# Batch 0's attention scores and exponentials kept in their PSUM bank up to the division, in a mixture-of-experts kernel

## Chip, cores, metric

One core of one Trainium2 chip runs the kernel. The metric is the device time of one execution in microseconds (us). The kernel before has a median of 1451.16 us over 3 runs (1449.22 to 1452.23).

## What is computed

Three stages follow one another: banded attention with 8 heads over 2 batches of 768 rows, a mixture of 8 experts whose weights come from a Sinkhorn iteration, and a gated feed-forward layer. Everything is fp32. The change touches the attention alone:

```python
scores = scale * np.matmul(q, k.transpose(0, 1, 3, 2))
...
scores = scores + bias[None, :, :, :]
scores = np.where(keep, scores, -1000000000.0)
scores = scores - np.max(scores, axis=-1, keepdims=True)
a = np.exp(scores)
a = a / (np.sum(a, axis=-1, keepdims=True) + 1e-09)
return np.matmul(a, v).astype(np.float32)
```

A row attends to its 96 nearest predecessors and to 8 global keys, so a tile of 128 queries needs two blocks of keys and 32 columns for the global keys.

## The kernel before

**Tiles.** The attention is cut into 2 batches x 4 pairs of heads x 6 tiles of 128 queries, 48 tiles in all. Tile 0 of a pair has 128 columns of scores for each head, tile 1 has 256, tiles 2 to 5 have 288 (`W`). `attention_banded` (L1084) makes one turn of its loop for each tile, and the letters of `ORDER` (L28) say in which order the steps of a turn are written into the engines' queues. Nothing reorders them afterwards. There are two ways of working: `self.phase` is 1 while attention runs alone (24 tiles of batch 0 and the first two of batch 1, turns 0 to 25), and 2 once the first expert layer's matmuls are interleaved with what is left of the attention.

**A turn of phase 1** has the order `tsvrn`. For turn n:

- `t`, `turn` (L1030), for the tile of turn n-3: PE transposes the weights `a` into the bank `pt` (L1039) and the 32 global columns into `pg` (L1047); ACT copies them to `ah` (L1042) and `ag` (L1051).
- `s`, `scores` (L978), for the tile of turn n, once for each of the pair's two heads j: three matmuls into a bank `s` (L1002); DVE adds the bias, scales and keeps the row's minimum in one pass, `tensor_tensor_reduce` (L1015; the trace calls it CUSTOM_DVE); ACT takes the exponential and sums the row into `rs` (L1018, followed by a read of its accumulator).
- `v`, `values` (L1066), for turn n-4: PE multiplies by the values (L1080), and after every second tile ACT copies the result out (L852).
- `r`: DVE subtracts to get the low part `al` (L1060) of turn n-3's transposed weights.
- `n`, `norm` (L1022), for turn n-1: DVE adds 1e-9 to the two row sums (L1025, called the epsilon step below), takes the reciprocal (L1026) and multiplies each head's weights by it (L1028, the two divisions).

After tiles 1 and 4 of each pair, `prep_qk` (L928) transposes the next half of the keys and queries: PE into `pk`, `pq`, ACT to `kh`, `qh` (L939, L949), DVE to `kl`, `ql` (L940, L950).

**PSUM.** There are eight banks: two for `s`, two for `t`, one for `v`, three for `m`. In phase 1 `psum` (L639) sends the scores to the three `m` banks, which nothing else uses then. A score bank of the kernel before comes free when DVE's pass L1015 has read it, since that pass writes to the SBUF tile `a`.

**POOL** splits the values and, in phase 1, the first expert weights and the first half of the layer's inputs (`split`, L207; `sum_weights`, L193), in one queue that runs beside the turns.

Of the kernel before, what the change touches and what calls it, by code (L numbers as in the profile page):

```python
# [12 lines left out]
ALU = mybir.AluOpType  # L13
# [3 lines left out]
P = 128  # L17
GK = 32
SLOT = P + GK
W = 2 * P + GK  # L20
# [28 lines left out]
class Kernel:  # L49
# [928 lines left out]
    def scores(self, b, hp, i):  # L978

        nc = self.nc  # L980
        qh, ql = self.aq[i // 3]

        pairs = lambda x, step: x.rearrange("p (s k) -> p s k", k=step)[:, :2, :P]
        if i == 0:
            keys, bias, wn = lambda x: x[:, :P], self.bias[:, W + P : W + 2 * P], P
        elif i == 1:
            keys, bias, wn = lambda x: pairs(x, SLOT), pairs(self.bias, W), 2 * P
        else:
            keys, bias, wn = lambda x: x[:, (i - 1) * SLOT : (i - 1) * SLOT + W], self.bias[:, P : P + W], W
        a = self.a_a.tile([P, 2, W], F32, tag="a", name=f"a_{b}_{hp}_{i}")  # L990
        rs = self.a_m.tile([P, 2], F32, tag="rs", name=f"rs_{b}_{hp}_{i}")

        rows = [slice(64 * j, 64 * j + 64) for j in range(2)]
        passes = [(ql, self.kh), (qh, self.kl), (qh, self.kh)]
        ps = {}

        def product(j, n):
            if n == 0:
                ps[j] = self.psum("s", [P, W], f"s_{b}_{hp}_{i}_{j}")[:, :wn]
            o = pairs(ps[j], P) if i == 1 else ps[j]  # L1000
            x, y = passes[n]
            nc.tensor.matmul(o, x[rows[j], i % 3, :], keys(y[rows[j]]), start=(n == 0), stop=(n == 2))  # L1002

        if self.phase > 1:
            for n in range(3):
                for j in range(2):
                    product(j, n)
        for j in range(2):
            if self.phase == 1:
                for n in range(3):  # L1010
                    product(j, n)
            s = a[:, j, :wn]
            o, x = (pairs(s, P), pairs(ps[j], P)) if i == 1 else (s, ps[j])
            m = self.a_m.tile([P, 1], F32, tag="m", name=f"m_{b}_{hp}_{i}_{j}")
            nc.vector.tensor_tensor_reduce(  # L1015
                out=o, in0=x, in1=bias, scale=-self.slope(2 * hp + j), scalar=3.0e38, op0=ALU.add, op1=ALU.min, accum_out=m
            )
            nc.scalar.activation(s, s, AF.Exp, bias=m, scale=-1.0, accum_out=rs[:, j : j + 1])  # L1018
            yield
        self.aa[b, hp, i] = a, rs, wn  # L1020

    def norm(self, b, hp, i):  # L1022
        nc = self.nc
        a, rs, wn = self.aa[b, hp, i]
        nc.vector.tensor_scalar(rs, rs, 1e-9, None, op0=ALU.add)  # L1025
        nc.vector.reciprocal(rs, rs)  # L1026
        for j in range(2):
            nc.vector.tensor_scalar(a[:, j, :wn], a[:, j, :wn], rs[:, j : j + 1], None, op0=ALU.mult)  # L1028

    def turn(self, b, hp, i):  # L1030

# [52 lines left out]
    def attention_banded(self):  # L1084

        nc = self.nc
        self.aq, self.av, self.vg = {}, {}, {}
        self.aa, self.at = {}, {}
        pairs = [(b, hp) for b in range(self.B) for hp in range(self.HP)]
        work = [(b, hp, i) for b, hp in pairs for i in range(self.NT)]  # L1090
        tables = self.tables()
        next(tables)
        self.scales()
        self.counts()
        next(tables)
        yield from self.prep_qk(0)
        next(tables)
        for n in range(len(work) + LV):
            b, hp, i = work[n] if n < len(work) else (None, None, None)
            pair = n // self.NT  # L1100
            rest = None
            for o in ORDER[self.phase]:
                if o == "s" and i is not None:
                    yield from self.scores(b, hp, i)
                    if n == 0:
                        self.prep_v(0)
                if o == "t" and LT <= n < len(work) + LT:
                    rest = self.turn(*work[n - LT])
                if o == "n" and 1 <= n <= len(work):
                    self.norm(*work[n - 1])  # L1110
                if o == "r" and rest is not None:
                    rest()
                    yield
                if o == "v" and n >= LV:
                    self.values(*work[n - LV])
                    yield work[n - LV]
            if i == 1:
                yield from self.prep_qk(2 * pair + 1)
            if i == 4 and pair + 1 < len(pairs):
                yield from self.prep_qk(2 * pair + 2)  # L1120
            if i == 2:
                self.prep_v(2 * pair + 1)
            if i == 5 and pair + 1 < len(pairs):
                self.prep_v(2 * pair + 2)
# [246 lines left out]
```

## Time and profile before

| | us |
|---|---|
| median of 3 runs | 1451.16 |
| the profiled execution | 1449.99 |
| its span, first to last instruction | 1448.2 |
| start of turn 0 on DVE | 12.3 |
| start of turn 26, the first of phase 2 | 97.2 |

The profile shows one execution. "Busy" of an engine is the sum of its instructions' times, and "idle before, <- X" is time in which the engine stood before an instruction until X released it. On DVE and ACT an instruction's time overlaps the next one's by about 0.08 us, so what an instruction costs in a queue is read from one start to the next. Starts in the timelines are us from the first instruction of the span.

### The profile page before, as it was taken

To read this page: it belongs to the slowest core of one execution; us is meant where nothing else is said; L and a number is where in the kernel's file an instruction comes from. 1 tells how busy PE (TensorE), PEld (TensorE's weight loads), DVE (VectorE), ACT (ScalarE), POOL (GpSimd) and SP (SyncE) were. 2 spreads that over 40 slices of the span, in tenths; PEclk is the share of its full clock that TensorE was granted. 3 is DMA by queue.
4 is the path that set the end of the run, shared out by engine and by line. 5 is a ranking of instruction groups with operands and counts; after the bars stand their busy time and mean duration, and the time that the engine had idled before them with its cause. 6 is when DMAs were issued, how large, how long until landed. Compare 5 with 4: busy or idle time off the path is not lost.

```text
span 1448.2 us, 20861 instructions
## 1 busy us (share of the span) xinstructions
PE 1403.7 (97%) x7295; PEld 1239.3 (86%) x7295; DVE 1002.1 (69%) x1881; ACT 638.6 (44%) x1528; POOL 851.6 (59%) x998
## 2 busy tenths in 40 slices
PE   7889999899999999999999999999999998999998
PEld 5568888788898998998998998998998977898997
DVE  7987886667767777777677777777655474556655
ACT  5676766343443343333343333343333365444332
POOL 4745555656885656554666554666554566566642
PEclk9999999999999999999999999999999999999999
DMA  6322210111231222221222221222100100010002
GB/s 160 79 50 63 74 48 30 59 59 59 70 113 59 74 80 88 73 74 51 87 75 87 74 71 54 84 77 88 44 30 29 44 16 30 30 44 30 30 1 88
DMA packets 92627, 89.55 MB, mean 62 GB/s; under 512 B 41824, under 2 KB 70496, under 8 KB 92512
## 3 DMA queue, kind: packets, MB, share of 16 engines
q1 hardware_dynamic: 92512, 88.12, 19.1%
q8 instruction: 60, 0.98, 0.3%
q14 instruction: 55, 0.45, 0.1%
HBM read 76.56 MB, written 11.53 MB: 61 GB/s over the span
## 4 chain that ended last, share of the span: by engine, by line
PE 83%; DVE 10%; ACT 4%; issue 2%; POOL 1%; POOLq 0%; DVEq 0%; ACTq 0%
PE pl L559 41%; PE pl1y L504 11%; PE pl1x L504 11%; PE pl1z L504 10%; PE pl1w L504 5%; PE pv L1080 2%; DVE hl L483 1%; PE s L1002 1%; DVE a L1028 1%; DVE u L456 1%; DVE a L1015 1%; DVE al L1060 1%; PE pt L1039 1%; ACT hh L480 1%; PE plg L374 0%
## 5 line engine op out<-in xcount | busy, mean ns | idle before, releaser
L570 DVE SCALAR_TENSOR_TENSOR acc<-pl,pr,acc 128x512 f32<-128x512 f32 x312 | 233.3, 749 | 117.0 <-PE pl L559 115.0
L559 PE MATMUL pl<-w2h,hl 128*128 128x512 f32 x960 | 301.5, 395 | 5.1 <-DVE accx L568 2.4
L559 PE MATMUL pl<-w2h,hh 128*128 128x512 f32 x960 | 298.1, 392 | 4.4 <-ACT hh L210 2.6
L559 PE MATMUL pl<-w2l,hh 128*128 128x512 f32 x960 | 297.6, 391 | 0.0
L216 POOL TENSOR_TENSOR w2l<-r,w2h 128x512 fp32r<-128x512 f32 x95 | 127.4, 1362 | 186.0 <-ACT w2h L210 174.6
L559 PEld LDWEIGHTS pl<-w2h,hh 128*128 128x128 f32 x960 | 180.3, 188 | 44.3 <-ACT hh L210 2.9
L559 PEld LDWEIGHTS pl<-w2l,hh 128*128 128x128 f32 x960 | 180.8, 188 | 39.4
L559 PEld LDWEIGHTS pl<-w2h,hl 128*128 128x128 f32 x960 | 176.5, 188 | 38.9 <-DVE accx L568 3.8
L210 ACT ACTIVATE w2h<-r 128x512 fp32r<-128x512 f32 x94 | 54.3, 625 | 194.0 <-PE pl L559 163.1
L478 POOL TENSOR_TENSOR hl<-u,hh 128x384 fp32r<-128x384 f32 x100 | 106.5, 1073 | 38.4 <-ACT hh L475 38.2
L478 POOL TENSOR_TENSOR hl<-p,hh 128x384 fp32r<-128x384 f32 x50 | 50.9, 1017 | 103.5 <-ACT hh L475 103.5
L511 ACT ACTIVATE p<-pl1x 128x384 f32<-128x384 f32 x80 | 39.2, 490 | 163.7 <-PE pl1x L504 156.5
L216 POOL TENSOR_TENSOR hl<-sg,hh 128x384 fp32r<-128x384 f32 x64 | 65.3, 1021 | 68.7 <-ACT hh L210 67.8
L456 DVE TENSOR_TENSOR u<-p,pl1y 128x384 f32<-128x384 f32 x86 | 47.4, 551 | 69.7 <-PE pl1y L504 63.7
L474 ACT ACTIVATE p<-p 128x384 f32<-128x384 f32 x50 | 26.3, 526 | 137.2 <-DVE p L456 137.2
L483 DVE SCALAR_TENSOR_TENSOR hl<-pl1x,hh 128x384 fp32r<-128x384 f32 x64 | 35.6, 556 | 68.8 <-ACT hh L480 68.5
L203 POOL TENSOR_TENSOR s<-r 128x256 f32<-128x256 f32 x96 | 77.7, 809 | 0.0
L216 POOL TENSOR_TENSOR S3l<-s,S3h 128x256 fp32r<-128x256 f32 x48 | 36.6, 762 | 69.9 <-ACT S3h L210 64.2
L474 ACT ACTIVATE u<-u 128x384 f32<-128x384 f32 x100 | 51.9, 519 | 49.4 <-DVE u L456 49.2
L1018 ACT ACTIVATE a<-a,m 128x288 f32<-128x288 f32 (+2 forms) x96 | 48.1, 501 | 41.0 <-DVE m L1015 41.0
L576 DVE TENSOR_TENSOR acc<-pl,acc 128x512 f32<-128x512 f32 x84 | 54.2, 681 | 13.7 <-PE pl L559 12.7
L456 DVE TENSOR_TENSOR u<-u,pl1w 128x384 f32<-128x384 f32 x74 | 40.8, 551 | 21.9 <-PE pl1w L504 21.2
(284 smaller groups left out, 3407.1 us busy)
## 6 DMA issues: line engine op xcount, KB each, us to landing
r<-in_moe_w_dram SPq DMA_DIRECT2D x80, 512.0 KB, 3.5
d<-in_moe_w_in_dram SPq DMA_DIRECT2D x16, 512.0 KB, 4.5
d<-cx SPq DMA_DIRECT2D x32, 256.0 KB, 2.4
d<-in_moe_w_out_dram SPq DMA_DIRECT2D x16, 512.0 KB, 4.2
r<-d SPq DMA_DIRECT2D x16, 512.0 KB, 3.7
out_dram<-acc SPq DMA_DIRECT2D x12, 256.0 KB, 2.1
k<-in_k_dram SPq DMA_DIRECT2D x28, 96.0 KB, 2.5
q<-in_q_dram SPq DMA_DIRECT2D x28, 96.0 KB, 2.5
```

The lines of the kernel that those rows point to most:

```text
L203: nc.gpsimd.tensor_tensor(out=o, in0=x, in1=y, op=op)
L210: nc.scalar.activation(hi, x, AF.Copy)
L216: e.tensor_tensor(out=lo, in0=x, in1=f(hi), op=ALU.subtract)
L456: add = lambda o, x, y: nc.vector.tensor_tensor(out=o, in0=x, in1=y, op=ALU.add)
L474: nc.scalar.activation(c, c, AF.Relu)
L478: nc.gpsimd.tensor_tensor(out=l, in0=c, in1=f(h), op=ALU.subtract)
L483: nc.vector.scalar_tensor_tensor(out=l, in0=c, scalar=0.0, in1=f(h), op0=ALU.max, op1=ALU.subtract)
L504: nc.tensor.matmul(ps, x[:, d, :], y[:, d, :], start=(new and i == 0 and d == 0), stop=(i == 2 and d == 1), skip_group_check=True)
L559: nc.tensor.matmul(ps, x[:, c, ts_], y, start=(n == 0 and c == 0), stop=(n == 2 and c == 1))
L570: nc.vector.scalar_tensor_tensor(out=acc, in0=ps, scalar=self.pr[:, tt, e : e + 1], in1=acc, op0=ALU.mult, op1=ALU.add)
L576: nc.vector.tensor_tensor(out=acc, in0=ps, in1=acc, op=ALU.add)
L1018: nc.scalar.activation(s, s, AF.Exp, bias=m, scale=-1.0, accum_out=rs[:, j : j + 1])
```

## The change

In phase 1 the scores plus bias overwrite the matmul's result in its own bank, the exponential overwrites them there, and the division reads the bank and writes the SBUF tile `a`, which is now written only there. The epsilon step writes its two sums into two spare columns of the second head's bank, and the reciprocal reads them there. `norm` of a tile that is kept in PSUM runs in that tile's own turn, behind `r`, and no longer in the next one. Phase 2 works as before. A score bank comes free when its division has read it.

```diff
         def product(j, n):
             if n == 0:
-                ps[j] = self.psum("s", [P, W], f"s_{b}_{hp}_{i}_{j}")[:, :wn]
+                t = self.psum("s", [P, W + 2], f"s_{b}_{hp}_{i}_{j}")
+                ps[j], ps["eps"] = t[:, :wn], t[:, W:]
...
-            s = a[:, j, :wn]
+
+            s = ps[j] if self.phase == 1 else a[:, j, :wn]
             o, x = (pairs(s, P), pairs(ps[j], P)) if i == 1 else (s, ps[j])
...
         self.aa[b, hp, i] = a, rs, wn
+        self.raw[b, hp, i] = ps if self.phase == 1 else None

     def norm(self, b, hp, i):
         nc = self.nc
         a, rs, wn = self.aa[b, hp, i]
-        nc.vector.tensor_scalar(rs, rs, 1e-9, None, op0=ALU.add)
-        nc.vector.reciprocal(rs, rs)
+        ps = self.raw.pop((b, hp, i))
+        eps = rs if ps is None else ps["eps"]
+        nc.vector.tensor_scalar(eps, rs, 1e-9, None, op0=ALU.add)
+        nc.vector.reciprocal(rs, eps)
         for j in range(2):
-            nc.vector.tensor_scalar(a[:, j, :wn], a[:, j, :wn], rs[:, j : j + 1], None, op0=ALU.mult)
+            x = a[:, j, :wn] if ps is None else ps[j]
+            nc.vector.tensor_scalar(a[:, j, :wn], x, rs[:, j : j + 1], None, op0=ALU.mult)
...
-                if o == "n" and 1 <= n <= len(work):
-                    self.norm(*work[n - 1])
+
+                for t in (n - 1, n):
+                    if o == "n" and 0 <= t < len(work) and work[t] in self.raw and (t < n or self.raw[work[t]]):
+                        self.norm(*work[t])
```

DVE's queue before, turn 5 and the first row of turn 6. In the names the first number is the pair of heads, the second the tile and, in `s` and `m`, the third the head; the last is a serial number. ISA is L1015's pass and the read of its accumulator:

```order
L1015 ISA a_0_5_19726,m_0_5_0_19732<-s_0_5_0_19728,bias 128x288
L1015 ISA m_0_5_0_19732 128x1
L1015 ISA a_0_5_19726,m_0_5_1_19739<-s_0_5_1_19735,bias 128x288
L1015 ISA m_0_5_1_19739 128x1
L1060 TENSOR_TENSOR al_0_2_19719<-pt_0_2_19713,ah_0_2_19718 128x512
L1025 TENSOR_SCALAR rs_0_4_19667<-rs_0_4_19667 128x2
L1026 RECIPROCAL rs_0_4_19667<-rs_0_4_19667 128x2
L1028 TENSOR_SCALAR a_0_4_19666<-a_0_4_19666,rs_0_4_19667 128x288 x2
L1015 ISA a_1_0_19778,m_1_0_0_19784<-s_1_0_0_19780,bias 128x128
```

The same place in the changed kernel:

```order
L1017 ISA s_0_5_0_19732,m_0_5_0_19736<-s_0_5_0_19732,bias 128x288
L1017 ISA m_0_5_0_19736 128x1
L1017 ISA s_0_5_1_19739,m_0_5_1_19743<-s_0_5_1_19739,bias 128x288
L1017 ISA m_0_5_1_19743 128x1
L1066 TENSOR_TENSOR al_0_2_19723<-pt_0_2_19717,ah_0_2_19722 128x512
L1030 TENSOR_SCALAR s_0_5_1_19739<-rs_0_5_19731 128x2
L1031 RECIPROCAL rs_0_5_19731<-s_0_5_1_19739 128x2
L1034 TENSOR_SCALAR a_0_5_19730<-s_0_5_0_19732,rs_0_5_19731 128x288
L1034 TENSOR_SCALAR a_0_5_19730<-s_0_5_1_19739,rs_0_5_19731 128x288
L1017 ISA s_1_0_0_19784,m_1_0_0_19788<-s_1_0_0_19784,bias 128x128
```

The norm behind `al` is now that of tile 5, whose scores stand five rows above it, where it was that of tile 4.

PE's queue before, at the scores of the first tile of the second pair:

```order
L1047 MATMUL pg_0_3_19773<-ident,a_0_3_19637 32x128 [waits DVE_49]
L1047 MATMUL pg_0_3_19773<-ident,a_0_3_19637 32x128
L1002 MATMUL s_1_0_0_19780<-kh,ql_19702 128x128
L1002 MATMUL s_1_0_0_19780<-kl,qh_19701 128x128
L1002 MATMUL s_1_0_0_19780<-kh,qh_19701 128x128
L1002 MATMUL s_1_0_1_19787<-kh,ql_19702 128x128
L1002 MATMUL s_1_0_1_19787<-kl,qh_19701 128x128
L1002 MATMUL s_1_0_1_19787<-kh,qh_19701 128x128
L1080 MATMUL pv_0_2_19794<-al_0_2_19719,vh_19544 128x256 [waits PE_49,Activation_49]
```

The same place in the changed kernel:

```order
L1053 MATMUL pg_0_3_19777<-ident,a_0_3_19641 32x128 [waits DVE_49]
L1053 MATMUL pg_0_3_19777<-ident,a_0_3_19641 32x128
L1003 MATMUL s_1_0_0_19784<-kh,ql_19706 128x128
L1003 MATMUL s_1_0_0_19784<-kl,qh_19705 128x128
L1003 MATMUL s_1_0_0_19784<-kh,qh_19705 128x128
L1003 MATMUL s_1_0_1_19791<-kh,ql_19706 128x128 [waits DVE_49]
L1003 MATMUL s_1_0_1_19791<-kl,qh_19705 128x128
L1003 MATMUL s_1_0_1_19791<-kh,qh_19705 128x128
L1086 MATMUL pv_0_2_19798<-al_0_2_19723,vh_19544 128x256 [waits Activation_49]
```

The order is the same, and the second head's first score matmul has a wait for DVE that it didn't have: its bank is the one that the tile before used for its first head.

## Rows read from the trace of the kernel before

**Rows 1.** The page, part 1: busy time and share of each engine over the whole span
```profile
PE 1403.7 (97%) x7295; PEld 1239.3 (86%) x7295; DVE 1002.1 (69%) x1881; ACT 638.6 (44%) x1528; POOL 851.6 (59%) x998
```

**Rows 2.** Windows, six turns each (last two turns): length, busy us of each engine, clock
```profile
12.30:26.20 13.90, 13.35 (x76) 10.31 (x77) 12.71 (x52) 11.12 (x36) 5.12 (x11) 1.00 0.70 204
26.20:44.00 17.80, 16.84 (x124) 12.53 (x122) 16.50 (x59) 14.71 (x46) 8.65 (x16) 1.00 0.56 116
44.00:66.60 22.60, 17.43 (x122) 12.29 (x120) 22.18 (x60) 14.48 (x45) 19.12 (x29) 0.99 0.32 77
66.60:88.40 21.80, 20.77 (x117) 14.92 (x118) 17.59 (x60) 15.30 (x45) 9.60 (x15) 0.78 0.31 79
88.40:97.20 8.80, 7.92 (x53) 6.11 (x53) 7.71 (x21) 7.11 (x21) 7.98 (x13) 1.00 0.30 69
```

**Rows 3.** Groups by shape, DVE, 12 to 97.3 us: count | busy us, mean ns | idle before
```profile
L1028 DVE TENSOR_SCALAR a<-a,rs 128x288 f32<-128x288 f32 x32 | 16.4, 553 | 0.6
L1015 DVE CUSTOM_DVE_ANT_0 a<-s,bias 128x288 f32<-128x288 f32 x33 | 13.8, 450 | 1.9 <-PE s L1002 1.7
...
L1025 DVE TENSOR_SCALAR rs<-rs 128x2 f32<-128x2 f32 x25 | 8.2, 327 | 0.0
L950 DVE SCALAR_TENSOR_TENSOR ql<-pq,qs,qh 128x384 fp32r<-128x384 f32 x9 | 5.5, 610 | 0.2 <-ACT qh L949 0.2
L940 DVE TENSOR_TENSOR kl<-pk,kh 128x384 fp32r<-128x384 f32 x9 | 5.0, 552 | 3.2 <-ACT kh L939 3.2
```

**Rows 4.** Timeline of DVE, 50 to 53 us: start, us taken, instruction
```profile
50.29 0.44 DVE L1015 CUSTOM_DVE_ANT_0 a<-s,bias 128x288 f32<-128x288 f32 x1
...
51.04 0.68 DVE L1060 TENSOR_TENSOR al<-pt,ah 128x512 fp32r<-128x512 f32 x1
51.65 0.44 DVE L1025 TENSOR_SCALAR rs<-rs 128x2 f32<-128x2 f32 x1
...
52.32 2.58 DVE L1028 TENSOR_SCALAR a<-a,rs 128x256 f32<-128x256 f32 x2
```

**Rows 5.** Timeline of POOL, 53 to 55 us
```profile
52.95 1.80 POOL L216 TENSOR_TENSOR B11l<-xf,B11h 128x768 fp32r<-128x768 f32 x1
```

**Rows 6.** Timeline of DVE, 20.8 to 22.4 us, POOL idle
```profile
20.80 0.69 DVE L1060 TENSOR_TENSOR al<-pt,ah 128x512 fp32r<-128x512 f32 x1
21.41 0.16 DVE L1025 TENSOR_SCALAR rs<-rs 128x2 f32<-128x2 f32 x1
...
21.80 0.65 DVE L1028 TENSOR_SCALAR a<-a,rs 128x288 f32<-128x288 f32 x2
22.37 0.55 DVE L940 TENSOR_TENSOR kl<-pk,kh 128x384 fp32r<-128x384 f32 x1
```

**Rows 7.** Timeline of ACT, 50.7 to 52 us
```profile
50.77 0.54 ACT L1018 ACTIVATE a<-a,m 128x288 f32<-128x288 f32 x1 [0.36 <-DVE m L1015]
...
51.73 0.19 ACT L1018 ACTIVATION_READ_ACCUMULATOR a<-a,m 128x1 f32 x1
```

**Rows 8.** Timeline of PE, 20 to 32 us
```profile
20.32 0.41 PE L1080 MATMUL pv<-ah,vl 128*128 128x256 f32 x1
...
27.27 0.66 PE L1039 MATMUL pt<-ident,a 128*128 128x128 f32 x4
...
29.20 0.28 PE L1080 MATMUL pv<-ah,vl 128*128 128x256 f32 x1
...
29.53 0.69 PE L1080 MATMUL pv<-ag,vg 32*128 32x256 f32 x2
...
31.62 0.41 PE L1002 MATMUL s<-kh,ql 64*128 64x288 f32 x2
...
31.99 0.30 PE L1002 MATMUL s<-kh,qh 64*128 64x288 f32 x2
```

**Rows 9.** The page, part 5: two ACT copies of 128x384, from PSUM and from SBUF
```profile
L511 ACT ACTIVATE p<-pl1x 128x384 f32<-128x384 f32 x80 | 39.2, 490 | 163.7 <-PE pl1x L504 156.5
...
L474 ACT ACTIVATE p<-p 128x384 f32<-128x384 f32 x50 | 26.3, 526 | 137.2 <-DVE p L456 137.2
```

More of the change, by code (lines that the diff above doesn't have):

```diff
@@ L1087, in attention_banded @@
         self.aq, self.av, self.vg = {}, {}, {}
-        self.aa, self.at = {}, {}
+        self.aa, self.at, self.raw = {}, {}, {}
         pairs = [(b, hp) for b in range(self.B) for hp in range(self.HP)]
```

## The prediction, as put on record before the changed kernel ran

> **What bounds the kernel now.** I read the page's busy times first. PE is busy for 97% of the span [rows 1], so over the whole run time is PE's. But the change acts only on turns 0 to 25, the 84.9 us from 12.3 to 97.2, and there it is otherwise. The windows by six turns (one pair of heads each) show it [rows 2]. In the second six, PE is busy 16.84 of 17.80 us: PE's bound, and about the least that six turns take. In the third six the same PE work takes 22.6 us, and DVE is busy for 22.18 of them: DVE's bound. In the fourth, 21.8 us, the clock column has 0.78 for PE, so part of that stretch ran at the lower of PE's two clocks, 1.2 GHz.
>
> What made DVE slow in the third six is in the groups by shape [rows 3]. The division over 288 columns has a mean of 553 ns and the epsilon step on two numbers 327, while in a quiet turn two divisions together take 0.65 us and the epsilon step 0.16 [rows 6]. DVE's pass over the scores, also 288 wide, reads PSUM and has a mean of 450 that equals its quiet time (0.44 in the middle of the busy stretch [rows 4]). The timelines tell why. Two divisions that began at 52.32 took 2.58 us [rows 4], to 54.90; POOL's subtraction began at 52.95 and ended at 54.75 [rows 5]. A DVE instruction that reads and writes SBUF with one tensor operand stands still while POOL works. I take it that one whose tensor operand is in PSUM does not, as the pass and `al` don't.
>
> **What the change removes.** These stalls. The 32 divisions of 288 columns cost 16.4 us, of which 32 x 0.325 (half of the quiet pair) = 10.4 is their quiet cost, so 6 us are stall; the 25 epsilon steps cost 8.2, quiet 4.0, so 4 more. Most lies in the third six turns.
>
> **What it adds.** Three things.
>
> (1) The division reads PSUM. The nearest row that reads PSUM with one operand per partition is `ql`: 610 ns for 384 columns, against 552 for `kl`, which has no such operand [rows 3]. Between `kl` (384) and the pass (288, 450 ns) lie 1.06 ns a column. So a division from PSUM takes 450 + 58 = 0.51 us and 0.43 from start to start, against (22.37 - 21.80)/2 = 0.285 now [rows 6]. That is 0.145 more, twice a turn. Ends: 0 and 0.145; I take 0.145.
>
> (2) A new wait. The division is now in its own tile's turn, so the epsilon step waits for the second head's exponential. In a 288-wide turn the first pass starts at 50.29, ACT's first exponential at 50.77, and its second sum is read at 51.73 + 0.19 = 51.92 [rows 4, 7]: 1.63 us after the turn's start. DVE gets there after two passes (51.04 - 50.29 = 0.75) and `al` (21.41 - 20.80 = 0.61), at 1.36. It waits about 0.3, with the second tile's passes and PE's `values` queued behind it.
>
> (3) A bank is freed by the division, so the second head's score matmuls wait for the first head's division of the turn before. Six score matmuls take 32.29 - 31.62 = 0.67 us on PE [rows 8], three some 0.55; in that time DVE does the second division and the first pass, 0.43 + 0.37. No wait for DVE then, except where PE itself is late.
>
> So a 288-wide turn takes 1.66 + 0.39 (epsilon to division [rows 6]) + 0.86 = 2.9 us on DVE. A 128-wide one has 160 columns less in one pass, in two exponentials (0.13 each) and in two divisions (0.17 each): 2.15. The 256-wide one takes 2.8, but PE's turn before it, some 2.95 us (27.27 to 30.22 [rows 8]), outlasts DVE's 2.15, and its `kl` waits for ACT; I add 0.9. `kl` and `ql` come twice in six turns at 1.0. Six turns: 4 x 2.9 + 2.15 + 3.7 + 2.0 = 19.45 us.
>
> **The sum**, against the windows [rows 2]:
> - turns 0 to 5: 13.9 becomes 19.0. In the first three there is no `al` to cover the exponentials (0.9 us of wait each), the first two turns can't overlap with PE's next ones, and PE is slow until about 22 us (a matmul of 256 columns takes 0.41 against 0.28 later [rows 8], though the clock column shows 1.00 there). Turn by turn 2.1, 4.1, 2.9, 3.0, 3.9, 2.9: **+5.1**.
> - turns 6 to 11: 17.8 becomes 19.45: **+1.65**. PE's slack now hides the division; DVE's new waits don't hide.
> - turns 12 to 17: 22.6 becomes 19.45 + 0.87 for a subtraction of the layer's inputs in turn 16: **-2.3**.
> - turns 18 to 23: 21.8 becomes 19.45 + 0.5 for input splits that ACT now does ahead of an exponential that DVE waits for: **-1.85**, with PE at 2.4 GHz throughout.
> - turns 24, 25: 8.8 becomes 2.65 + 5.1 (`kl` waits for ACT as now): **-1.05**; turn 26 loses its norm, of which I count **-0.5**, as PE bounds it.
> - the exponentials read PSUM. ACT's copy of 384 columns takes 490 ns from PSUM and 526 from SBUF [rows 9], so 0.036 less, twice a turn, in some 20 turns that wait for them: **-1.4**.
>
> In all -0.4 us. The profiled execution took 1449.99 and lies 1.2 below the median; I set the sum against the median and say 1451 us, no measurable change. A measurement of this kernel can tell about 0.2% from no change, 2.9 us. POOL's queue (17 us of work between turns 10 and 16) fits in those turns' 19 to 20 us, and SP issues the same transfers; both cost nothing. From turn 27 on nothing is changed, and the rest moves with the end of turn 26.
>
> The Trainium skill (ScalarE: Activation LUTs, "Step-by-step: what each stage is for") says that ScalarE also writes to PSUM sooner than to SBUF. No row here shows such a write; if it gave another 0.036 us each time, the sum would be -1.8.
>
> **Rivals.**
>
> *Faster: the division keeps its pace in PSUM.* If it ran at 0.285 from PSUM too, or if the exponentials were shorter still, a turn would take 2.6 and not 2.9, and with about 22 turns that DVE sets the sum would be -0.4 - 22 x 0.29 = -6.8: 1444. For it: no row shows this instruction reading PSUM. Against it: 288 columns in 0.285 us are less than 1.06 ns a column, so the SBUF form runs more than one column at a time, and no row that reads PSUM does. Halfway, 1447.5, it would already count as faster. The same side is reached if the first six turns lose only half of my 5.1 us. Together 0.32. The Trainium skill (VectorE: DVE Perf Modes, "Why PSUM operands drop a tier") speaks against the change here: an fp32 operand in PSUM holds the instruction to one element a cycle. By that rule this rival falls and (1) stands at 0.145.
>
> *Slower: PE's gaps keep it at 1.2 GHz.* PE stood for several us between 53 and 65 us (it was busy for 17.4 of 22.6 us in those six turns) and then ran at the lower clock in the fourth six. There the mean of 0.78 over 21.8 us means 9.6 us at half speed, 4.8 us of PE time lost. After the change PE has to wait in nearly every turn: 16.8 us of work in 19.45. If the rise that came at about 22 us comes 10 us later, because the first turns are thinner, or if the fall in the fourth six stays, PE and no longer DVE sets these turns. Each such stretch costs up to 4.8: 1455.5, two 1460. It decides once some 3 us of six turns run at half speed: PE's 16.8 us of work then outlast DVE's 19.45. 0.17.
>
> *Slower: working in place in one bank costs.* No row shows DVE reading and writing the same PSUM bank. Ends: nothing, and a second run over the columns, 288 x 1.06 = 0.31 for each pass, 0.6 a turn, 16 us: 1467. The PSUM rows here have no extra time over SBUF, so I take nothing; a quarter of it would give 1455. 0.11.
>
> *The change doesn't free DVE from POOL.* If writing SBUF or reading the two sums there were enough for the stall, the 6 + 4 us would stay and the new waits come on top: about 1457. Against it: `al` writes SBUF and takes 0.68 us in the busy stretch as in the quiet one [rows 4, 6]. 0.04.
>
> No change as summed: 0.36. So faster 0.32, same 0.36, slower 0.32. The range: 1444.5, near the faster rival's end, to 1459, which takes in one or two slow-clock stretches and a quarter of the in-place cost. The likeliest case alone is 1448.3 to 1454.1.
>
> **What would show it.** In the changed profile: the divisions near 510 ns and the epsilon step near 160 at every place, however busy POOL is; DVE idle before the epsilon step on ACT's accumulator, 0.3 us in most turns and 0.9 in turns 0 to 2; PE waiting for the division ahead of the second head's scores; turn 6 starting at 31 and not at 26.2 us, turn 12 at 51, turn 18 at 71, turn 26 near 98. The forecast is wrong if the pass over the scores lengthens, if turns 6 to 11 take under 18.5 or over 20.5 us, or if PE's clock is low between 25 and 97 us.

## The result and the profile after

The changed kernel is slower. Its median is 1461.03 us over 5 runs (1458.79 to 1472.07), against 1450.63 us for the kernel before in the same session: a ratio of 1.0088, 95% interval 1.0070 to 1.0106. The forecast of 1451.0 us was wrong, and its range, which ended at 1459, missed the median too. The profiled execution took 1463.36 us, its span 1461.5. Its mean clock of PE is 0.987 where the median execution has 0.991, and the five executions go with that clock: 1458.8 us at 0.992, 1472.1 at 0.981. So the profile shows somewhat more low clock than the median has.

The windows of the changed kernel by six turns (length, busy us of PE, PEld, DVE, ACT, POOL, clock of PE, share and rate of DMA) answer to [rows 2]:

```profile
12.79:33.65 20.86, 17.38 (x72) 13.53 (x72) 15.71 (x57) 11.34 (x36) 6.23 (x13) 1.00 0.72 187
33.65:53.57 19.92, 18.42 (x122) 13.65 (x121) 17.26 (x59) 14.19 (x45) 6.93 (x14) 1.00 0.22 51
53.57:77.46 23.89, 22.42 (x122) 16.76 (x121) 18.10 (x60) 14.31 (x45) 18.25 (x28) 0.79 0.30 73
77.46:100.63 23.17, 22.14 (x122) 16.50 (x121) 17.29 (x59) 15.25 (x47) 10.01 (x17) 0.78 0.31 75
100.63:108.93 8.30, 8.30 (x56) 6.48 (x56) 5.83 (x21) 6.99 (x21) 7.89 (x13) 1.00 0.20 46
```

The 26 turns take 96.1 us for 84.9. That is 11.2 of the 13.3 us by which the two profiled spans differ. The third and fourth row tell why they are long: DVE is busy for only 18.10 of 23.89 us, where it had 22.18 of 22.60, and PE for 22.42. The clock column has 0.79 and 0.78. At half speed that is (1 - 0.79) x 2 x 23.89 = 10.0 us of low clock and 10.2, where the kernel before had 9.6 in the fourth stretch alone.

DVE's groups by shape (12 to 109 us; count | busy us, mean ns | idle before) answer to [rows 3]:

```profile
L1034 DVE TENSOR_SCALAR a<-s,rs 128x288 f32<-128x288 f32 x32 | 15.1, 513 | 0.6
L1017 DVE CUSTOM_DVE_ANT_0 s<-s,bias 128x288 f32<-128x288 f32 x32 | 14.1, 471 | 5.5 <-PE s L1003 5.4
...
L1017 DVE DVE_READ_ACCUMULATOR2_ANT m<- 128x1 f32 x52 | 7.3, 141 | 0.0
...
L1030 DVE TENSOR_SCALAR s<-rs 128x2 f32<-128x2 f32 x26 | 4.3, 164 | 6.9 <-ACT s L1020 6.6
```

The stalls beside POOL are gone: the division has 513 ns, the epsilon step 164. In place in the bank the pass has a mean of 471 ns for 450. The read of its accumulator takes 141 ns for 81, and ACT's exponential, in the bank too, 471 for 528. The kernel before (DVE 12 to 97 us, ACT 12 to 102), then the changed one (ACT 12 to 102):

```profile
L1015 DVE DVE_READ_ACCUMULATOR2_ANT m<- 128x1 f32 x52 | 4.2, 81 | 0.0
...
L1018 ACT ACTIVATE a<-a,m 128x288 f32<-128x288 f32 x36 | 19.0, 528 | 14.7 <-DVE m L1015 14.7
```

```profile
L1020 ACT ACTIVATE s<-s,m 128x288 f32<-128x288 f32 x32 | 15.1, 471 | 17.4 <-DVE m L1017 17.4
```

The timeline of DVE in one turn at full clock (start, us, instruction, idle before):

```profile
40.72 0.46 DVE L1017 CUSTOM_DVE_ANT_0 s<-s,bias 128x288 f32<-128x288 f32 x1
...
42.37 0.16 DVE L1030 TENSOR_SCALAR s<-rs 128x2 f32<-128x2 f32 x1 [0.18 <-ACT s L1020]
42.57 0.17 DVE L1031 RECIPROCAL rs<-s 128x2 f32<-128x2 f32 x1
42.77 0.94 DVE L1034 TENSOR_SCALAR a<-s,rs 128x288 f32<-128x288 f32 x2
43.63 0.46 DVE L1017 CUSTOM_DVE_ANT_0 s<-s,bias 128x288 f32<-128x288 f32 x1
```

A turn lasts 43.63 - 40.72 = 2.91 us, as forecast. The places where PE stands still for over 0.2 us between 43 and 78 us:

```profile
43.35 0.40 PE L1003 MATMUL s<-kh,ql 64*128 64x288 f32 x1 [0.46 <-DVE a L1034]
52.19 0.39 PE L1053 MATMUL pg<-ident,a 128*32 128x128 f32 x2 [0.81 <-DVE al L1066]
53.28 0.32 PE L1003 MATMUL s<-kh,ql 64*128 64x128 f32 x1 [0.23 <-DVE a L1034]
64.75 0.40 PE L1003 MATMUL s<-kh,ql 64*128 64x288 f32 x1 [0.45 <-DVE a L1034]
76.08 0.39 PE L1053 MATMUL pg<-ident,a 128*32 128x128 f32 x2 [0.80 <-DVE al L1066]
77.18 0.32 PE L1003 MATMUL s<-kh,ql 64*128 64x128 f32 x1 [0.23 <-DVE a L1034]
```

Windows of 3 us set beside them show where the clock falls:

```profile
52.00:55.00 3.00, 2.59 (x16) 1.99 (x16) 2.70 (x12) 2.57 (x10) 2.83 (x6) 1.00 0.12 26
55.00:58.00 3.00, 3.00 (x16) 2.00 (x15) 1.17 (x6) 0.85 (x2) 2.78 (x7) 0.59 0.21 46
58.00:61.00 3.00, 3.00 (x20) 2.38 (x18) 2.23 (x9) 2.19 (x8) 2.80 (x5) 0.84 0.00 0
61.00:64.00 3.00, 3.00 (x20) 2.07 (x19) 2.67 (x9) 2.53 (x9) 2.92 (x3) 1.00 0.70 159
64.00:67.00 3.00, 2.55 (x13) 1.94 (x12) 2.49 (x10) 1.27 (x5) 2.49 (x5) 0.80 0.72 201
67.00:70.00 3.00, 3.00 (x13) 1.74 (x13) 1.13 (x4) 1.35 (x3) 0.00 (x0) 0.50 0.03 12
```

After the gaps at 52 and 53 us the clock is low in the next window; after the gap at 64.75 it falls within the same window. But the gap at 43.35, as long as that one, is not followed by a fall: the clock is 1.00 up to 55 us. In the low stretches PE never pauses, and DVE waits for it ahead of the next tile's first pass:

```profile
57.60 0.43 DVE L1017 CUSTOM_DVE_ANT_1 s<-s,bias 128x256 f32<-128x256 f32 x1 [1.79 <-PE s L1003]
...
69.87 0.47 DVE L1017 CUSTOM_DVE_ANT_0 s<-s,bias 128x288 f32<-128x288 f32 x1 [1.83 <-PE s L1003]
```

PE's own work is longer too, at full clock already: 18.42 us in turns 6 to 11 where it was 16.84. The kernel before runs the score matmuls of a tile's two heads side by side, 64 rows each, six of them in 0.67 us [rows 8]. Where the second head's bank is still held, each head's three run alone:

```profile
42.23 0.40 PE L1003 MATMUL s<-kh,ql 64*128 64x288 f32 x1
42.47 0.29 PE L1003 MATMUL s<-kl,qh 64*128 64x288 f32 x1
42.60 0.28 PE L1003 MATMUL s<-kh,qh 64*128 64x288 f32 x1
43.35 0.40 PE L1003 MATMUL s<-kh,ql 64*128 64x288 f32 x1 [0.46 <-DVE a L1034]
```

Three take 0.65 us, nearly as long as six did. The 36 score matmuls of six tiles keep PE busy for 5.91 us (32.5 to 52.4 us, clock 1.00), for 3.86 in the kernel before (25.0 to 42.5 us, clock 1.00).

So the theory was: the new waits leave PE short gaps, its clock falls to 1.2 GHz, and PE's work for a turn then outlasts DVE's. The rivals: the waits cost the time themselves and the clock only goes along; or an instruction that works in place in a bank costs more on the path than its row shows.

### The profile page after: what moved, and what is told of

Read it like the earlier page. It is cut to its first block, busy times and chain, and to the rows that moved or that the text cites. A ratio compares the mean times of both kernels' runs of the same rounds, so it can differ in the third digit from the quotient of the medians.

```text
span 1461.5 us, 20874 instructions
## 1 busy us (share of the span) xinstructions
PE 1417.8 (97%) x7295; PEld 1251.1 (86%) x7295; DVE 997.7 (68%) x1881; ACT 637.9 (44%) x1528; POOL 849.5 (58%) x998
## 4 chain that ended last, share of the span: by engine, by line
PE 84%; DVE 9%; ACT 4%; issue 2%; POOL 1%; POOLq 0%; DVEq 0%; ACTq 0%
PE pl L559 41%; PE pl1x L504 11%; PE pl1y L504 10%; PE pl1z L504 10%; PE pl1w L504 5%; PE pv L1086 2%; PE s L1003 2%; DVE hl L483 1%; DVE u L456 1%; PE pt L1045 1%; DVE a L1034 1%; ACT s L1020 1%; ACT hh L480 1%; PE plg L374 0%; POOL s L203 0%
## 5 line engine op out<-in xcount | busy, mean ns | idle before, releaser
L456 DVE TENSOR_TENSOR p<-u,pl1z 128x384 f32<-128x384 f32 x74 | 40.8, 551 | 21.7 <-PE pl1z L504 20.2
```

Of the source, the lines that this page charges most:

```text
L456: add = lambda o, x, y: nc.vector.tensor_tensor(out=o, in0=x, in1=y, op=ALU.add)
```

## Experiments

Each median stands against the kernel before in the same session (1449.9 to 1451.3 us).

### The own-turn order alone, from SBUF

```diff
+        self.own[b, hp, i] = self.phase == 1
...
-                if o == "n" and 1 <= n <= len(work):
-                    self.norm(*work[n - 1])
+                for t in (n - 1, n):
+                    if o == "n" and 0 <= t < len(work) and work[t] in self.own and (t < n or self.own[work[t]]):
+                        self.own.pop(work[t])
+                        self.norm(*work[t])
```

> The kernel before with one part of the change alone: in phase 1 the norm runs in its own tile's turn; scores and exponentials go to SBUF as before, so banks come free early and the stalls behind POOL stay. Theory 'own turn': the wait for the exponential alone lengthens it to 1457 or more. Theory 'clock': without the bank wait PE runs ahead and the time is 1451 to 1455.

Measured: 1460.46 us, ratio 1.0063 (1.0039 to 1.0087). Moving the norm, with nothing in the bank, costs nearly the whole loss. PE stands still longer here (up to 2.71 us at a time, for 0.81 in the changed kernel), and the clock is low in the three windows of turns 6 to 23:

```profile
32.94:53.42 20.48, 18.00 (x117) 13.12 (x118) 17.80 (x59) 14.77 (x44) 7.89 (x15) 0.91 0.22 50
53.42:78.38 24.96, 20.47 (x116) 15.00 (x115) 20.77 (x61) 14.91 (x44) 17.94 (x27) 0.77 0.28 68
78.38:99.59 21.21, 18.97 (x118) 13.44 (x117) 17.45 (x59) 14.85 (x45) 9.71 (x15) 0.87 0.33 81
```

### More banks for the scores

Two versions take five banks (three `m`, two `s`) and send the transposes of keys and queries to the `t` banks; two take four and leave them in `s`. Of each pair one norms in the own turn, one in the next (with four banks the second tile of each pair stays in its own turn). The banks of the first two, then of the last two:

```diff
-        elif self.phase == 1:
-            kind = {"s": "m", "p": "s"}.get(kind, kind)
+        elif self.phase == 1 and kind == "s":
+            kind = "mmmss"[self.scored % 5]
+            self.scored += 1
...
-            kind = {"s": "m", "p": "s"}.get(kind, kind)
+            self.scored += kind == "s"
+            kind = {"s": "smmm"[self.scored % 4], "p": "s"}.get(kind, kind)
```

Five banks, own turn:

> The changed kernel with five score banks in place of three (the keys' and queries' transposes move to the two transpose banks), so that the second head's score matmuls no longer wait for a division; the norm stays in its own tile's turn. Theory 'clock' (PE's waits for the division thin its work, it falls to 1.2 GHz in phase 1 and then sets the turns): the low-clock stretches before turn 26 shrink to 10 us or less and the time is 1450 to 1455. Theory 'own turn' (the wait of the epsilon step for the exponential makes the turns long whatever PE does): turns 6 to 23 still take 60 us or more and the time stays at 1458 or above.

Five banks, next turn:

> As the run with five banks, and the norm goes back to the next tile's turn (tile 25's alone is still in its own), so neither new wait is left; scores, exponentials and epsilon step stay in PSUM. If the stalls behind POOL were worth what the trace of before says, six turns come near PE's 17 us and the time is 1440 to 1446, below both kernels, on either theory. If taking the transposes of keys and queries into the transpose banks costs as much as the stalls did, 1449 to 1452.

Four banks, own turn:

> The changed kernel with four score banks in batch 0 instead of three (every second tile's second head takes one of the other score pool's two), the preparation of keys and queries where it was. The second head's scores no longer wait for the division of the tile before (5.7 us in 9 places between 12 and 103 us in the changed kernel); the epsilon step still waits for its own tile's second exponential (6.0 us in 20 places). If the waits themselves are the loss: 5 to 6 us come back, 1455 to 1456 us. If the loss is PE's clock, which falls because the own-turn wait leaves PE gaps: the gaps stay, 14 us or more of low clock before 103 us, and 1458 to 1461 us.

Four banks, next turn:

> As the one with four banks, but each tile is normed in the next tile's turn as before the change (from the bank), only every sixth tile, after which keys or queries are prepared, in its own. Neither the bank wait nor, in five tiles of six, the wait for the exponential is left, and no epsilon step runs beside a POOL instruction on SBUF. If the loss comes from the own-turn wait and what it does to PE's clock: six turns as short as before the change or shorter, at most 7 us of low clock before 100 us, and 1447 to 1452 us. If operations that read and write the same bank are dearer on the path than their rows show (pass 471 ns for 450, its accumulator read 141 ns for 81): still 1455 to 1458 us. If PE's clock falls for another reason than the waits: 1457 us or more with over 10 us of low clock.

Measured: 1461.81 us (1.0065 to 1.0121), 1457.53 (1.0033 to 1.0089), 1467.51 (1.0062 to 1.0131) and 1467.27 (1.0090 to 1.0173). The first came out as the theory of the own turn had it: its turns 6 to 23 took 65.7 us, with low clock only in turns 12 to 17 (0.93). The second and third lie in none of the ranges named for them; the fourth lies where its clock was to fall for another reason than the waits. Each brought a wait of its own. PE's waits (line waited for: us, times, longest) of five banks in the own turn, and of four in the next turn, show it:

```profile
PE pt L1046 <- DVE kl L941: 11.3, 8, 2.4
```

```profile
PE pq L945 <- DVE a L1035: 14.3, 8, 3.0
```

The longer hold on the banks only changes who waits: the transposes of the weights behind `kl`, or those of the queries behind the division. So these runs don't tell the theories apart. They do show that PE's pauses alone don't say when the clock falls: with five banks and the norm in the next turn PE worked 17.84 of 21.12 us in turns 6 to 11 and kept its clock there:

```profile
30.04:51.16 21.12, 17.84 (x119) 12.66 (x119) 16.87 (x58) 14.29 (x44) 7.48 (x14) 1.00 0.28 62
```

### Unread matmuls (fillers) in every turn

```diff
+                if j == 1:
+                    self.filler()
...
+    def filler(self):
+        d = self.psum("p", [P, W], "fill")
+        for _ in range(4):
+            self.nc.tensor.matmul(d, self.fz[:, :P], self.fz, start=True, stop=True)
```

> The changed kernel with four matmuls of 288 columns that nobody reads (0.12 us each at 2.4 GHz, 12.5 us in all) put into PE's queue in each turn of phase 1, just ahead of the second head's score matmuls, where PE waits for the division. Theory 'clock': PE stays at 2.4 GHz through turns 6 to 25 and the time falls, to 1450 to 1456, in spite of the added work. Theory 'own turn' or 'bank wait alone': the same 1461 or up to 8 us more.

With two instead of four:

> The changed kernel with two unread 128x288 matmuls ahead of the second head's scores in each turn (their output goes nowhere), half of the four that held the clock but stood in the path with 0.75 us. Two take 0.3 to 0.4 us, about the gap of 0.46 us in which PE waits there for the division. If the clock is what costs the 10 us: where the two keep it at full through batch 0's 26 tiles, 1453 to 1457 us in spite of the added work; where it still falls, 1460 us or more and low stretches in the record. If the waits cost it and the clock only goes along: the added work makes it 1463 us or more even at full clock.

Measured: 1474.62 us (ratio 1.0152 to 1.0229) and 1473.56 (1.0144 to 1.0243). With two of them, turns 12 to 17:

```profile
58.32:81.56 23.24, 22.41 (x133) 16.50 (x132) 18.62 (x61) 14.88 (x45) 18.35 (x28) 1.00 0.31 75
```

The clock holds, but PE is now the bound by its own added work: 22.41 us, where the changed kernel at full clock had 18.42 in six turns. Both times lie outside what the theory of the clock allowed, and by its words the second speaks for the waits; with PE loaded like this neither run gives the price of the clock.

### Unread matmuls only where PE stood still

```diff
+                if i == 3 and j == 1:
+                    self.filler(3)
                 for n in range(3):
                     product(j, n)
...
+        if i == 3 and self.phase == 1:
+            self.filler(5)
         if i >= 2:
             pg = self.psum("t", [GK, 2, P], f"pg_{b}_{hp}_{i}")
```

> The changed kernel with unread matmuls (128x288, their output goes nowhere) placed only where its PE stands still between 25 and 100 us: five ahead of the fourth tile's pg transposes (PE waits there 0.80 us at 52.2 and at 76.1 us), three ahead of the fourth tile's second head's scores (0.45 us at 43.4, 64.8 and 88.6 us). In the trace each of the four low stretches of the clock begins within 2 us of such a place. They take about 0.65 and 0.4 us, so nearly nothing on the path. If PE's clock, brought down by these gaps, is what the prediction missed: low stretches before 100 us shrink from 20 us to 7 or less, the six-turn lengths 23.9 and 23.2 become 20 to 21.5, and 1453 to 1457 us. If the falls have another cause: they stay and the time is 1460 us or more. If the waits are the loss and the clock only goes along: the falls go and the time stays at 1459 us or more.

Measured: 1455.08 us over 6 runs (1454.30 to 1457.11), ratio 1.0042 (1.0030 to 1.0055). Adding eight matmuls to each pair of heads gave back 6 of the 10 us. (Its expectation has the low stretches begin within 2 us of such a place. Two began 1 us after a gap ahead of the scores; the other two began 3.4 us after the gap ahead of `pg`, 2.3 us after the short one that follows it.) The windows by six turns:

```profile
12.40:32.50 20.10, 17.80 (x80) 14.06 (x80) 15.69 (x56) 11.35 (x36) 5.47 (x12) 1.00 0.72 188
32.50:52.49 19.99, 19.58 (x130) 14.66 (x129) 17.32 (x59) 14.21 (x45) 7.74 (x15) 1.00 0.25 56
52.49:73.25 20.76, 19.71 (x130) 14.66 (x129) 18.15 (x61) 14.33 (x45) 18.33 (x29) 1.00 0.34 84
73.25:93.36 20.11, 19.61 (x130) 14.66 (x129) 17.35 (x59) 15.00 (x47) 10.02 (x17) 1.00 0.35 86
93.36:101.67 8.31, 8.31 (x56) 6.50 (x56) 5.84 (x21) 6.99 (x21) 7.89 (x13) 1.00 0.20 45
```

DVE, ACT and POOL are busy as long as in the changed kernel, in the third and fourth rows to within 0.3 us. The clock column differs, 1.00 for 0.79 and 0.78, and PE's busy time with it, and the two rows shrink from 23.89 and 23.17 to 20.76 and 20.11. The 26 turns take 89.3 us. So in this execution 20.2 us of low clock cost 6.2 us in these twelve turns, 0.31 us for each us. The own-turn wait is still there (DVE stands 6.6 us for the exponentials in the 26 turns of either kernel), so it is not what cost these 6 us. At full clock PE is the bound of these turns: 19.58 of 19.99 us in turns 6 to 11.

The change in tiles 12 to 25 alone:

```diff
-            s = ps[j] if self.phase == 1 else a[:, j, :wn]
+            s = ps[j] if self.phase == 1 and hp >= 2 else a[:, j, :wn]
...
-        self.raw[b, hp, i] = ps if self.phase == 1 else None
+        self.raw[b, hp, i] = ps if self.phase == 1 and hp >= 2 else None
```

> The change only in tiles 12 to 25 of batch 0, where POOL stalls DVE's SBUF steps; tiles 0 to 11 are normed in the next turn from SBUF as before the change. By the prediction's terms at full clock the first twelve turns take 31.7 us again and the rest 20.3, 20.0 and 7.8 us for 22.6, 21.8 and 8.8: 5.2 us less than before, near 1446 us. If PE's clock falls in tiles 12 to 25 as in the changed kernel (23.9 and 23.2 us): 1450 to 1454 us. If the loss is the own-turn wait everywhere alike, with the clock no matter: 1454 to 1456 us, half of the whole.

and with the same fillers:

> The change only in tiles 12 to 25, with the unread matmuls of the run before last at the fourth tile of each pair. If the gaps bring the clock down and the clock is the loss: full clock in tiles 12 to 25 and 1445 to 1449 us, below the kernel before and below the same without them. If they only add work: as without them or up to 2 us more.

Measured: 1457.78 us (ratio 1.0028 to 1.0068) and 1454.62 (1.0022 to 1.0044). Both miss their ranges, and neither gets under the kernel before. With fillers the median is 3 us lower, but the two intervals overlap. The ten executions without fillers form a scale of the clock within one kernel: the two whose mean granted clock was 0.993 took 1451.2 and 1451.6 us, the seven at 0.986 to 0.988 took 1454.6 to 1459.2, the one at 0.983 took 1465.6. Even at 0.993 nothing is gained over the kernel before. The profiled execution with fillers is one of the two longest of its ten (1458.4 us). Its turns 18 to 23 have full clock and take 20.10 us, but turns 12 to 17 lost theirs in spite of the same fillers:

```profile
48.92:77.43 28.51, 27.25 (x123) 20.04 (x121) 19.70 (x65) 14.54 (x44) 18.37 (x28) 0.64 0.26 62
77.43:97.53 20.10, 19.61 (x130) 14.64 (x129) 17.35 (x59) 14.99 (x47) 10.02 (x17) 1.00 0.35 86
```

### The kernel before, without its epsilon step and with fillers

The sums are at least 1, and 1e-9 leaves them as they are.

```diff
-        nc.vector.tensor_scalar(rs, rs, 1e-9, None, op0=ALU.add)
         nc.vector.reciprocal(rs, rs)
```

> The kernel before the change without the epsilon step (the exponentials' sums are at least 1, and 1e-9 more leaves such a float32 as it is). It takes out 32 steps of 327 ns mean in batch 0, 10.5 us of DVE, most of it waiting beside POOL. If DVE's stalls are what spaces the turns of the kernel before: 1444 to 1448 us. If the reciprocal, which also writes SBUF, takes the stall over, or if PE and the exponentials space the turns: 1449 to 1452 us. If shorter DVE turns leave PE gaps that cost its clock: above 1453 us.

With fillers ahead of the fourth tile's `pg`, and then the same fillers with the step kept:

> The kernel before the change, without the epsilon step and with five unread 128x288 matmuls ahead of the fourth tile's pg transposes in batch 0, where PE waited 1.9 us at 63.6 us in the run without the step, ahead of 13.7 us of low clock in which six turns took 23.5 us where the six before took 20.7. If the clock is lost at that gap: six turns of 20.5 to 21.5 us, 1445 to 1447 us. If not, 1448 to 1450 us as without them.

> The kernel before the change with five unread 128x288 matmuls ahead of the fourth tile's pg transposes in batch 0, the epsilon step kept. Without that step the same fillers brought 4 us (1448.9 to 1444.8 us). If it is the clock there too: the 10 us of low clock at 66 to 76 us shrink and 1446 to 1448.5 us. If DVE's waits beside POOL hide the clock's fall in the kernel before, as they set the pace of its turns 12 to 17: 1449.5 to 1451.5 us, with or without the fall.

Measured: 1448.87 us without the step (ratio 0.9979 to 1.0001, which is not told from no change), 1444.75 with fillers too (0.9950 to 0.9980), 1447.22 with fillers alone (0.9972 to 0.9991). Turns 12 to 17 and 18 to 23 without the step, then turns 0 to 5 and again 12 to 23 with fillers alone:

```profile
44.22:64.89 20.67, 16.79 (x118) 12.07 (x117) 19.18 (x54) 14.41 (x45) 19.25 (x29) 0.98 0.35 84
64.89:88.36 23.47, 22.43 (x120) 16.29 (x120) 16.09 (x53) 15.18 (x47) 10.26 (x16) 0.73 0.29 73
```

```profile
12.35:26.25 13.90, 13.55 (x80) 10.77 (x81) 12.72 (x52) 11.05 (x36) 5.13 (x11) 1.00 0.73 207
...
44.19:66.77 22.58, 20.34 (x127) 15.20 (x126) 22.16 (x61) 14.43 (x45) 19.10 (x29) 0.85 0.32 78
66.77:85.23 18.46, 17.15 (x122) 12.29 (x122) 17.18 (x60) 14.77 (x45) 9.55 (x15) 1.00 0.36 92
```

Without the step DVE is 3 us less busy in turns 12 to 17 and these are 1.9 us shorter, but then the clock falls further (0.73 for 0.78) and 1.7 us go again. With fillers the fall comes earlier, in turns where DVE is busy for 22.16 of 22.58 us and hides it, and turns 18 to 23 take 18.46 us and not 21.8. So the low stretch of the kernel before cost it 3.3 us there, and the medians give 3.0.

### The two halves, both with fillers

The own-turn order from SBUF, with fillers ahead of the third and fourth tile's `pg`:

> The kernel before the change with the norm in its own tile's turn and the division still from SBUF to SBUF, with seven unread 128x288 matmuls (about 0.95 us) ahead of the pg transposes of the third and fourth tile of each pair, where PE stood still 0.3 to 2.7 us without them. It parts the change's two halves at full clock: against the changed kernel with fillers (1455.1 us, 89.3 us for 26 turns) only the bank is missing, so DVE's epsilon step and divisions wait beside POOL again. If the bank takes those waits out of the path and nothing else: 1 to 4 us longer, 1456 to 1459 us. If the bank gains nothing at equal clock, for the second head's scores wait for the division: 1453 to 1455.5 us. If its clock still falls, the run decides nothing.

Measured: 1464.63 us (ratio 1.0072 to 1.0116). The third tile's fillers stood behind `kl` for 9.7 us, in the bank they share with the preparation; the run decides nothing. Then those were put ahead of the transposes, in their own bank:

```diff
+        if i == 2 and self.phase == 1:
+            for _ in range(8):
+                nc.tensor.matmul(pt[:, 0].rearrange("p j t -> p (j t)"), self.fz[:, :P], self.fz[:, : 2 * P], start=True, stop=True)
```

> The run with the own-turn order from SBUF again, but the fillers of the third tile go into its own transposes' bank ahead of the transposes (eight of 128x256), for in the run before they stood behind the keys' subtraction for 9.7 us. Against the changed kernel with fillers (1455.1 us; 26 turns in 89.3 us) only the bank is missing. If the bank takes DVE's waits beside POOL out of the path: 1456 to 1459 us at held clock, the most of it in turns 12 to 17 (22 to 23.5 us for 20.8). If it gains nothing at equal clock: 1453 to 1455.5 us. If the clock falls again by over 10 us before 100 us, undecided.

Measured: 1455.20 us over 10 runs (1454.07 to 1456.29), ratio 1.0028 (1.0018 to 1.0038). Without the bank the time is the same within the noise (1.0030 to 1.0055 with it). The windows show a gain of the bank that is given back:

```profile
12.40:32.08 19.68, 17.87 (x98) 14.60 (x99) 15.85 (x57) 11.34 (x36) 6.55 (x13) 1.00 0.72 189
32.08:50.79 18.71, 17.32 (x132) 13.49 (x130) 16.74 (x59) 14.51 (x44) 7.04 (x13) 1.00 0.29 65
50.79:74.33 23.54, 21.80 (x137) 17.16 (x136) 21.72 (x60) 14.56 (x44) 19.08 (x29) 0.85 0.31 74
74.33:93.86 19.53, 17.80 (x130) 13.36 (x130) 17.42 (x59) 14.62 (x45) 9.71 (x15) 1.00 0.36 88
93.86:101.89 8.03, 8.03 (x55) 6.29 (x54) 6.62 (x21) 7.28 (x22) 7.46 (x11) 1.00 0.22 51
```

Against the run with the bank and fillers, turns 12 to 17 are 2.8 us longer (23.54 for 20.76; DVE is busy 21.72 for 18.15). The other stretches are shorter by 0.4, 1.3, 0.6 and 0.3, together 2.6 us. The clock fell once here, in turns 12 to 17 (0.85, some 7 us); DVE is busy for most of that stretch, but part of the 2.8 us may be PE's. With that clock held too the version without the bank should only be faster, and it carries more fillers (fifteen for each pair, for eight), so these runs give the bank no gain. What gives it back is PE's part above all: without the bank the two heads' score matmuls run side by side again (3.86 us in turns 6 to 11, for 5.83), and PE is busy for 17.32 of 18.71 us there, where with the bank it is for 19.58 of 19.99.

Last, the version that had been fastest, with fillers at both places (six and seven):

> The kernel before the change without the epsilon step, with fillers at both places of PE's gaps: seven ahead of the fourth tile's pg transposes, six of 128x256 ahead of the third tile's transposes in their bank. The one with five at the first place alone took 1444.8 us and still lost its clock for 6.8 us after gaps of 0.8 to 1.0 us at 57 to 62 us. If the clock holds there too: 1442 to 1444.5 us. If PE has no room for the more work: 1445 to 1448 us.

Measured: 1446.02 us, ratio 0.9964 (0.9948 to 0.9979). It is no better than five at the one place. The fastest version is the kernel before without the epsilon step and with those five: 1444.75 us, below both kernels.

## Why the prediction was wrong

**The terms for DVE held.** The division from PSUM was forecast at 0.51 us and took 513 ns; the epsilon step near 160, 164; the wait for the exponential 0.3, and it was 0.18 in a usual turn and 0.44 behind a short `al`; a 288-wide turn 2.9, and it was 2.91. The Trainium skill (VectorE: DVE Perf Modes, "Why PSUM operands drop a tier") holds an fp32 instruction with an operand in PSUM to one element a cycle; 513 ns against the quiet pair's 0.65 for two [rows 6] agrees, and the rival in which the division keeps its pace fell. The exponential had a mean of 471 ns, 528 in the kernel before: 0.057 less, where 0.036 was taken. Two of the prediction's signs of being wrong came all the same: the pass lengthened (471 ns for 450), and PE's clock was low between 25 and 97 us.

**The step that failed** is the one for turns 18 to 23, "with PE at 2.4 GHz throughout", and with it the same tacit assumption for turns 12 to 17. They were forecast at 19.95 and 20.3 us and took 23.17 and 23.89. With the gaps filled they took 20.11 and 20.76, so 3.1 us in each are the clock. That is the rival "PE's gaps keep it at 1.2 GHz", which had 0.17, and PE did set these turns, as it says. Its time for two stretches was 1460, and 1461 was measured, but this nearness is luck: its price was too high (up to 4.8 us a stretch, 3.1 measured), and the rest of the loss is an error of the sum. Nor do some 3 us at half speed decide, as it has it: 16.8 us of work outlast 19.45 only after 5.3 us at half speed. Some 10 us were measured in each stretch.

The same step hid a second error. The forecast gain of 1.85 us in turns 18 to 23 was reckoned against 21.8 us, of which 3.3 were the kernel before's own low clock. At full clock on both sides the change costs 1.65 us there (20.11 for 18.46).

**The sum at held clock** was 4.2 us too low: 89.3 us for 26 turns, where the five stretches of the forecast add up to 86.45, and to 85.05 with the 1.4 us that it took off for the exponentials. (Its turns 0 to 5 add up to 18.9, not 19.0.) The first six took 20.1 and not 19.0; PE's matmuls ran slow for longer there than before the change, by the 256-column matmuls of `values`, which take 0.28 us from 23.5 us on in the kernel before and still 0.41 at 31.0 in the changed one. The clock column has 1.00 there in both, so that it is the clock is not shown. The rest is 0.15 to 0.55 us in each of the other stretches and the 1.4. Here term (3) failed, which has the second head's scores come later and cost nothing: it kept PE's work at 16.8 us for six turns, and with the heads apart it was 18.42.

**Where the 10 us went,** by these runs: the own-turn order costs 1455.2 - 1447.2 = 8.0 us with fillers on both sides (the clock fell to 0.85 in turns 12 to 17 of both), 5.8 of it in the first six turns (19.68 for 13.90; 19.65 without any fillers), for which the prediction had 5.1. Some of the rest may be the ten fillers for each pair that the own-turn version has more. The bank gains nothing (1455.1 for 1455.2). The clock costs the changed kernel 1461.0 - 1455.1 = 5.9 us, and the kernel before loses 1450.2 - 1447.2 = 3.0. So 8.0 + 5.9 - 3.0 = 10.9, for 10.4 measured. These differences chain the same medians, so that they add up confirms nothing; each is as good as its own pair of runs.

**The other rivals.** Work in place in a bank does cost DVE 21 ns a pass and 60 ns (141 for 81) a read of the accumulator, together 52 x 81 ns = 4.2 us of DVE's time. The prediction took nothing for it; 81 ns is about the quarter of a second run over the columns (0.31 us) that it priced at 1455. How much of it is on the path no run shows: with the gaps filled PE, not DVE, is busy for nearly all of turns 6 to 11 and 18 to 23. That the change does not free DVE from POOL is refuted by the 513 and 164 ns.

## What to carry to other kernels

A wait that was moved onto a nearly full PE cost more than its length here, by the clock and by matmuls that no longer ran side by side: first price the bound at both of PE's clocks, and ask of each low stretch in the trace before whether the change would end it or repeat it. Before a faster engine is credited with the time of a stretch, hold the clock in both versions, here with a few unread matmuls in PE's own gaps, and compare those. Banks held longer moved their wait to whatever shared the banks in all four versions here, and what freeing an engine gained in one stretch (2.8 us) was paid back in all the others, above all by the heads that the held bank set apart on PE.

## What the runs showed of the hardware

- PE lost its clock although it never stood still for more than 0.81 us at a time between 25 and 100 us, and eight unread matmuls for each pair of heads, some 1.1 us in 20, kept it at 2.4 GHz in the profiled execution. What exactly decides is open: with five score banks PE paused more and kept its clock in turns 6 to 11; with the fillers in place a gap of 0.70 us at 68 us was not followed by a fall; and with the change in tiles 12 to 25 alone the same fillers did not hold the clock (0.64 in turns 12 to 17). The Trainium skill (TensorE: Matmul & The Clock Gate, "A second HAM failure mode: psum-queue depth-cycling") tells of a kernel whose matmuls cycle through PSUM banks and pause so often that the clock swings between its levels. The changed kernel's trace agrees in kind, with the clock at 0.79 and 0.78 of full and three banks in turn. That the banks are the cause is not shown: with the scores in SBUF, where a bank is held no longer than before the change, the clock fell as well (0.77).
- Two matmuls of 64 rows each, on different rows, run side by side: six of 288 columns in 0.67 us, and three by themselves in 0.65.
- More work can be faster: the kernel before gained 3 us from five unread matmuls a pair, although its clock still fell, only in a place that DVE hides.
- DVE's read of the accumulator after a pass that writes PSUM takes 141 ns, 81 after one that writes SBUF; ACT's exponential in place in PSUM is 57 ns shorter than in SBUF.
